# Down projection by 26 products of a 4x4 by 4x2 scheme, with gate and up products accumulated onto copies in PSUM

## The chip, the cores and the metric

One Trainium2 chip, one of its NeuronCores. A core has TensorE (PE, with PEld its weight loads), VectorE (DVE), ScalarE (ACT), GpSimd (POOL) and SyncE (SP, which issues most DMAs); they run their own instruction streams in order and meet through semaphores. The metric is the device time of one launch in microseconds.

## The reference

Two blocks read the same x (2048 tokens, 576 features); a sigmoid gate mixes them.

```python
B, S, D = 1, 2048, 576          # Df = 4608
x = A_x
g = sigmoid((x * gate_w).sum(-1, keepdims=True))
a = linear_attention(x, wqkv) @ wo      # 32 heads of 18
b = (gelu(x @ w_gate) * (x @ w_up)) @ w_down
return g * a + (1 - g) * b
```

All inputs and the result are float32.

## The kernel before

Float32 accuracy comes from splitting each operand into a high and a low part of type fp32r: `hi` is an ACT copy, `lo` is the raw value minus `hi`, made by DVE or POOL. A product is then hi·hi + hi·lo + lo·hi, three matmuls for each 128 rows of the contraction.

The program has three stages. The first (to about 243 us) is the attention block; it leaves g·a in DRAM (`ga_d`) and is written out step by step in the string `PLAN`. The second is **gate/up** (`gu_steps`, matmuls on L801), the third **down** (`unit`, matmuls on L1065). `manual_schedule` means that each engine's order is the order in which the Python code issues, so the order in the loops is the order on the chip.

*Gate/up.* The 2048 tokens are two halves p of 1024; each half is a 2x2 matrix of blocks (512 tokens by 288 features). The weight columns are taken 256 at a time, n = 0 to 17, again as 2x2 blocks. A **chain** (p, n, m), with m GATE or UP, multiplies the two by Winograd's scheme in 7 products (`PRODUCTS`), each of 7 matmuls of 128x512 into one PSUM bank. There are 72 chains (`CHAINS`), for each n in the order GATE half 0, GATE half 1, UP half 0, UP half 1, one after the other: `s1, s6, s7, s5, s2, s4, s3`. What the scheme adds between products is done by ACT and DVE on the way out: `s1` copies its bank to `p1` (L844), `s6` and `s7` add to it from their banks (L849, L863: `u2`, `u3`), `s5`, `s4`, `s3` add again (L835, L838), then GELU for GATE (L825, L855) or a multiplication into `es[i]` for UP (L828). So no product of PE waits for another engine, except for a free bank. `es` are four blocks of 512 tokens by 128 features; half 0 has `e...`, half 1 has `f`. After UP, four more sums (L877, L878, L879, L889) form the left operands of the down scheme, and `keep_block` (L831) stores all seven to DRAM (`h_d`).

Weights of the next n are fetched by SP (L805, 768 KB); POOL makes the four sums of the scheme (L321, 128x384 each), ACT the high parts (L815), POOL the low parts (L816, and 32 rows in L817). `w_split` and `w_fetch` stand behind the first product of a chain.

*Down.* h (1024 tokens of a half by 768 features) times the matching rows of w_down, as 2x2 by 2x2 blocks, again in 7 products: 6 steps s, 2 halves, 7 products, 84 **units**. A unit is four token tiles t of 9 matmuls, 128x288. Its left operand comes from DRAM (`h_load`, 768 KB) and is split by ACT and DVE (`h_make`, L966 and L967), three units ahead; its right operand is split by ACT and POOL (`d_make`, L946 and L948, in two pieces of 432) after POOL's `d_sum` (L953) made the scheme's sums. Each right operand serves both halves, so there are 42. Results go from PSUM into the accumulators `acc` in SBUF by DVE with the factor 1-g (L1073): `acc += bank * gate`, in 288 instructions; product 1 is copied to a second bank by ACT (L1069) and both are added to. In the sequence 1, 6, 2, 7, 5, 4, 3 the products use the banks a, b, a, b, d, b, d.

```python
    for u, (s, p, k) in enumerate(UNITS):
        unit(u, 0)          # token tiles 0, 1
        ...                 # h_make(u + 3), h_load(u + 6)
        unit(u, 1)          # token tiles 2, 3
```

## Time and profile before

| | |
|---|---|
| median of 3 runs | 1470.54 us (1469.54 to 1472.34) |
| the profiled execution (span) | 1470.6 us |
| busy: PE, PEld, DVE, ACT, POOL | 1465.0, 1311.9, 1038.5, 547.2, 720.9 us |
| gate/up stage | about 243 to 1066 us, 3528 matmuls of L801 |
| down stage | about 1066 to 1470.6 us, 3024 matmuls of L1065 |
| HBM | 156.84 MB read, 88.28 MB written |

The profile is one execution. Busy time of an engine is time in which an instruction of it ran; PEld overlaps PE. A group's row ends in `busy us, mean ns of one | idle time before them`, with what ended that idle time. A timeline row is `start, length, engine, line, operation, out<-in, count`.

### The profile page before, as it was taken

The page shows a single profiled execution, that of the slowest core. Times are in us where ns is not written, and L with a number is a line of the kernel's source. Part 1 is how long each engine was busy: PE and PEld are TensorE (multiplying, and loading weights), DVE is VectorE, ACT ScalarE, POOL GpSimd, SP SyncE. Part 2 cuts the span into 40 slices and gives each one's busy share as a digit, 9 for nine tenths or more (in the row PEclk, how much of TensorE's full clock was granted, in tenths as well). Part 3 has the DMA queues.
Part 4 walks back from the last instruction along what each step waited for, and adds up shares of the span by engine and source line. Part 5 has one row for each costly group of instructions (what it writes and reads, how often), then busy time and mean ns, then how long its engine had stood idle before and what let it go on. Part 6 is the DMA issues. An engine that isn't in the chain of part 4 may idle for free.

```text
span 1470.6 us, 21605 instructions
## 1 busy us (share of the span) xinstructions
PE 1465.0 (100%) x8312; PEld 1311.9 (89%) x8312; DVE 1038.5 (71%) x1351; ACT 547.2 (37%) x719; POOL 720.9 (49%) x522
## 2 busy tenths in 40 slices
PE   9999999999999999999999999999999999999999
PEld 9999899888888888888888888888899999999999
DVE  7887898565677655677665677665778777777775
ACT  7555656333322223222223222232254444443431
POOL 1664543456455464465464464462446464463710
PEclk9999999999999999999999999999999999999999
DMA  7564476653333222333222333224796655565563
GB/s 255 160 207 140 161 250 218 238 220 129 108 143 143 108 103 108 112 143 144 94 107 107 123 143 126 103 109 182 263 344 213 218 173 204 169 221 199 175 215 127
DMA packets 100599, 246.56 MB, mean 168 GB/s; under 512 B 9416, under 2 KB 36616, under 8 KB 98320
## 3 DMA queue, kind: packets, MB, share of 16 engines
q1 hardware_dynamic: 97760, 237.91, 46.6%
q10 hardware_dynamic: 2736, 7.28, 1.3%
q8 instruction: 65, 1.06, 0.3%
q14 instruction: 38, 0.31, 0.1%
HBM read 156.84 MB, written 88.28 MB: 167 GB/s over the span
## 4 chain that ended last, share of the span: by engine, by line
PE 98%; DMA 1%; DVE 1%; ACT 0%; SPq 0%; issue 0%; DVEq 0%
PE bank L801 54%; PE bank L1065 27%; PE bank L479 4%; PE pair L728 4%; PE pair L282 2%; PE kpair L282 2%; PE pair L237 2%; PE kpair L237 2%; PE den L667 1%; DMA xn<-xn 0%; DMA raw<-wk 0%; PE pair L634 0%; PE pair L530 0%; DVE e L246 0%; ACT pkh L252 0%
## 5 line engine op out<-in xcount | busy, mean ns | idle before, releaser
L801 PE MATMUL bank<-xo,wg 128*128 128x512 f32 x1764 | 403.7, 389 | 0.0
L801 PEld LDWEIGHTS bank<-xo,wg 128*128 128x128 f32 x1764 | 330.8, 188 | 68.9 <-DVE f L835 0.3
L801 PE MATMUL bank<-xo,wu 128*128 128x512 f32 x1715 | 391.8, 389 | 0.0
L801 PEld LDWEIGHTS bank<-xo,wu 128*128 128x128 f32 x1715 | 321.9, 188 | 66.8
L1073 DVE SCALAR_TENSOR_TENSOR acc<-bank,gate,acc 128x288 f32<-128x288 f32 x288 | 139.9, 512 | 67.1 <-PE bank L1065 64.8
L321 POOL TENSOR_TENSOR stage<-stage 128x384 f32<-128x384 f32 x132 | 153.7, 1185 | 49.0 <-ACT ga L735 23.2
L844 ACT ACTIVATE p<-bank 128x512 f32<-128x512 f32 x72 | 43.0, 597 | 325.2 <-PE bank L801 204.9
L816 POOL TENSOR_TENSOR wg<-stage,wg 128x768 fp32r<-128x768 f32 (+3 forms) x37 | 73.8, 1996 | 164.8 <-ACT wg L815 163.3
L816 POOL TENSOR_TENSOR wu<-stage,wu 128x768 fp32r<-128x768 f32 (+1 forms) x34 | 76.5, 2251 | 141.7 <-ACT wu L815 140.4
L1065 PE MATMUL bank<-wd,xo 128*128 128x288 f32 x1008 | 136.2, 295 | 0.0
L1065 PEld LDWEIGHTS bank<-wd,xo 128*128 128x128 f32 x1008 | 134.4, 188 | 0.0
L948 POOL TENSOR_TENSOR xo<-stage,xo 128x432 fp32r<-128x432 f32 x44 | 65.0, 1498 | 112.7 <-ACT xo L946 84.0
L849 DVE TENSOR_TENSOR u<-bank,p 128x512 f32<-128x512 f32 x72 | 49.4, 686 | 89.0 <-PE bank L801 81.2
L1065 PE MATMUL bank<-xo 128*128 128x288 f32 x792 | 107.0, 295 | 0.2 <-DVE u L838 0.2
L1065 PEld LDWEIGHTS bank<-xo 128*128 128x128 f32 x792 | 105.6, 188 | 0.5 <-DVE u L838 0.4
L948 POOL TENSOR_TENSOR wd<-stage,wd 128x432 fp32r<-128x432 f32 x40 | 59.4, 1510 | 90.1 <-ACT wd L946 72.3
L835 DVE TENSOR_TENSOR f<-bank,u 128x512 f32<-128x512 f32 x54 | 37.2, 691 | 69.2 <-PE bank L801 68.8
L825 ACT ACTIVATE f<-f 128x512 f32<-128x512 f32 x54 | 34.1, 632 | 128.6 <-DVE f L835 128.6
L863 DVE TENSOR_TENSOR u<-bank,u 128x512 f32<-128x512 f32 x72 | 49.8, 692 | 38.1 <-PE bank L801 34.1
L953 POOL TENSOR_TENSOR stage<-stage 128x432 f32<-128x432 f32 x48 | 76.3, 1616 | 0.0
L825 ACT ACTIVATE e<-e 128x512 f32<-128x512 f32 x54 | 34.0, 631 | 91.9 <-DVE e L835 91.9
L835 DVE TENSOR_TENSOR e<-bank,u 128x512 f32<-128x512 f32 x54 | 37.1, 691 | 40.4 <-PE bank L801 39.0
(198 smaller groups left out, 2373.2 us busy)
## 6 DMA issues: line engine op xcount, KB each, us to landing
h_d<-sx SPq DMA_DIRECT2D x108, 256.0 KB, 7.7
stage<-wgu SPq DMA_DIRECT2D x34, 768.0 KB
xo<-h_d SPq DMA_DIRECT2D x29, 768.0 KB, 6.9
e<-h_d SPq DMA_DIRECT2D x28, 768.0 KB, 4.2
hraw<-h_d SPq DMA_DIRECT2D x27, 768.0 KB, 4.1
h_d<-e SPq DMA_DIRECT2D x72, 256.0 KB, 2.0
h_d<-f SPq DMA_DIRECT2D x72, 256.0 KB, 2.0
stage<-wdn SPq DMA_DIRECT2D x6, 1728.0 KB, 9.6
```

Of the source, the lines that this page charges most:

```text
L237: nc.tensor.matmul(out_t[:, :n], xa, kvw[i][:, r, lo:lo + n], start=(k == 0), stop=(k == 13))
L282: nc.tensor.matmul(y[:, n, :KH], a, p[:, n * KH:(n + 1) * KH], start=(k == 0), stop=(k == len(ops) - 1))
L321: nc.gpsimd.tensor_tensor(o, a, b, OP.subtract)
L479: nc.tensor.matmul(ps[:wa.shape[1]], wa, xa, start=(k == 0), stop=(k == len(ops) - 1), skip_group_check=g == 4)
L801: nc.tensor.matmul(ps, w_, x_, start=start and i == 0, stop=i == 6, skip_group_check=not start)
L816: nc.gpsimd.tensor_tensor(w[:, i, 3:5], src[:, :, 0:2], f32(w[:, i, 0:2]), OP.subtract)
L825: nc.scalar.activation(es[i], es[i], AF.Gelu_apprx_tanh)
L835: nc.vector.tensor_tensor(es[i], a, b, OP.add)
L948: nc.gpsimd.tensor_tensor(w[:, 1, c], src[:, c], f32(w[:, 0, c]), OP.subtract)
L953: nc.gpsimd.tensor_tensor(draw[:, o, c], draw[:, x, c], draw[:, y, c], OP.subtract)
L1065: nc.tensor.matmul(y, h[:, hl, g, t * 128:(t + 1) * 128], w[:, wl, g * 288:(g + 1) * 288], start=k in (1, 5) and n == 0, stop=n == len(ops ...
L1073: nc.vector.scalar_tensor_tensor(o, y, gate[:, 1, st:st + 1], o, op0=OP.mult, op1=OP.add)
```

## The change

*Down* is now one scheme for a 4x4 matrix of left blocks (4 token blocks of 512 by 4 feature blocks of 384) and a 4x2 matrix of right blocks: 26 products, listed in the string `DOWN`, in three chunks c over the features (`NK = 3`, 1536 each), so 78 units of 36 matmuls. A line of `DOWN` gives the left operand (a sum of stored blocks `a`, `b`), the right operand, whether the product goes on in the banks of the one before (`c`), starts afresh (`-`) or starts on a copy of an earlier product's sum (a number, made by ACT), which outputs it is read into with which sign, and which right operands are summed just before. The chunks and the products that go on accumulate in PSUM, so a set of four banks is read only where the scheme needs it: 24 reads of four tiles, 96 DVE instructions (L1350). A negative read uses `probe[:, 8:]` (g-1), a negative left operand the factor -1 in `h_make` (L1204). Each unit has a right operand of its own: 78 splits on POOL (L1174, one piece of 864), and 54 sums of 864 (L1168), 33 on DVE and 21 on POOL, 18 tiles `vt` for them; the four newest right blocks are fetched ahead (`weight.fetch`).

*Every left operand is stored by the up steps.* UP of n even (role 0, "a" blocks) and of n odd (role 1, "b" blocks) belong together; `extras` forms the sums, a block at a time, in fixed slots after the UP chain, stores them (L1004, L1010) and, for role 1, loads back the "a" sums of the even n (L1007). The sums (L992, L995) read two SBUF blocks.

*Gate/up chains* no longer keep `u2`, `u3` in SBUF: `seed` has ACT copy bank a to a new bank b after `s1`, and b to a new bank c after `s6` (L939), and products 6, 3 accumulate onto b, products 7, 4 onto c. What is left to add is product 5, copied by ACT to `d_sum` (L967) and added by DVE (L969, L979 for GATE; L972, L982 for UP, back into PSUM). Two chains are interleaved in frames of seven slots:

```diff
+        def seed(name, src, k):
+            o = ps[name] = bank()
...
+                nc.scalar.activation(o, src, AF.Copy)
...
+        def s1():
+            a = ps["a"] = bank()
+            product(p, 1, w, a, True)
+            seed("b", a, 6)
+
+        def s6():
+            onto("b", 6)
+            seed("c", ps["b"], 7)
...
+        def s5():
+            d = bank()
+            product(p, 5, w, d, True)
+            nc.scalar.activation(d_sum, d, AF.Copy)
+            if m == GATE:
+                nc.vector.tensor_tensor(es[3], ps["c"], d_sum, OP.add)
+                gelu(3)
...
+    FRAME = 1, 7, 5, 3, 6, 2, 4
...
+                step = begun.get(frame if FRAME[i] in (1, 6, 2) else frame - 1, {}).get(FRAME[i])
```

The weight split of a chain stands in slot 0 of the frame before, the next fetch in its slot 5; the half-1 operand pieces move:

```diff
-    S_AT = [(0, 4), (1, 3), (2, 4), (2, 6), (3, 1), (3, 3)]
+    S_AT = [(0, 4), (2, 0), (3, 1), (3, 3), (3, 5), (4, 0)]
...
+    for n in range(3, NF2):
+        split_at(4 * n - 3, 0, GATE, *ALL)
+        fetch_at(4 * n - 3, 5, n, UP)
+        split_at(4 * n - 1, 0, UP, *ALL)
+        if n < NF2 - 1:
+            fetch_at(4 * n - 1, 5, n + 1, GATE)
```

The extras of an UP chain of half 1 with n odd (keys are frame, counted from the chain's own, and slot; `do` sums and stores, `get` loads), and those of the last chain that run in down, two groups a unit (`late`):

```diff
+        return {(-1, 5): [get("7", r0), get("x", r1), get("y", r2)],
+                (0, 3): [get("6", e[0])],
+                (0, 4): [get("5", e[3])],
+                (0, 5): [do(add, e[1], e[1], f[0])],
+                (0, 6): [do(add, e[1], e[1], r0, "a7b7")],
+                (1, 0): [do(sub, e[0], e[0], f[0], "a6b6"), do(add, r0, r0, f[0], "a7b6")],
+                (1, 1): [do(sub, r2, f[0], r2, "ayb6")],
+                (1, 2): [do(add, s0, s0, f[3])],
...
+                (2, 0): [do(sub, e[2], f[2], e[2]), do(add, e[2], e[2], r2, "a9b9")],
+                (2, 1): [do(add, s2, s1, f[3], "by"), get("8", r1)],
```

Down's tables and loop, each shortened to what the steps need:

```diff
+DOWN = """
+-b0 30 - -10 .
+-b2 r c . y=21-31,r=y-30
...
+NK = 3
...
+    def h_make(j):
...
+            if all(minus for minus, _, _ in DOWN[UNITS[j][0]].parts):
+                nc.scalar.activation(h[:, 0], raw, AF.Copy, scale=-1.0)
+                nc.vector.scalar_tensor_tensor(h[:, 1], raw, -1.0, f32(h[:, 0]), op0=OP.mult, op1=OP.subtract)
...
+        def make(self, j):
+            m, c = UNITS[j]
+            w, src = wd[j % 4], self.tile(DOWN[m].v, c)
+            nc.scalar.activation(w[:, 0], src, AF.Copy)
+            nc.gpsimd.tensor_tensor(w[:, 1], src, f32(w[:, 0]), OP.subtract)
...
+            for minus, i, j in d.reads:
+                st, o = 4 * i + t, acc[:, i, j, t]
+                by = probe[:, 8 + st:9 + st] if minus else gate[:, 1, st:st + 1]
+                nc.vector.scalar_tensor_tensor(o, y, by, o, op0=OP.mult, op1=OP.add)
...
+    weight.fetch(7)
+    h_load()
+    acc_load(1)
+    for u in range(len(UNITS)):
         unit(u, 0)
...
+        h_make(u + 3)
+        w_make(u + 3)
+        w_sums(u + 4)
+        later()
         unit(u, 1)
```

How the order moves, at three places. First PE in the middle of gate/up, before (x49 is a chain of seven products; xo and xo_3216 are the operands of half 0 and half 1, wg and wu the gate and up weights):

```order
L801 MATMUL bank<-xo,wg 128x512 x49
L801 MATMUL bank<-xo_3216,wg 128x512 x49
L801 MATMUL bank<-xo,wu 128x512 x49
L801 MATMUL bank<-xo_3216,wu 128x512 x49
L801 MATMUL bank<-xo,wg 128x512 x49
```

and after (xo_3263 is half 1's operand):

```order
L854 MATMUL bank<-xo_3263,wu 128x512 x7
L854 MATMUL bank<-xo_3263,wg 128x512 x21
L854 MATMUL bank<-xo_3263,wu 128x512 x14
L854 MATMUL bank<-xo_3263,wg 128x512 x7
L854 MATMUL bank<-xo,wg 128x512 x7
L854 MATMUL bank<-xo_3263,wu 128x512 x21
L854 MATMUL bank<-xo,wg 128x512 x14
```

Each chain is now spread over two frames: products 1, 6, 2 in its own, 7, 5, 3, 4 between those of the next chain.

Second DVE, from the end of an UP chain of half 1 into the next GATE chain, before (u and p are the sums in SBUF, sx the sums for down):

```order
L828 TENSOR_TENSOR f<-u_2892,f 128x512
L877 TENSOR_TENSOR sx<-f 128x512
L878 TENSOR_TENSOR sx<-sx,f 128x512
L879 TENSOR_TENSOR f<-f 128x512
L838 TENSOR_TENSOR u_2891<-bank,u_2891 128x512
L828 TENSOR_TENSOR f<-u_2891,f 128x512
L889 TENSOR_TENSOR sx<-f,sx 128x512
L849 TENSOR_TENSOR u_2891<-bank,p_2890 128x512
L863 TENSOR_TENSOR u_2892<-bank,u_2891 128x512
L835 TENSOR_TENSOR e_3212<-bank,u_2892 128x512 x2
```

and after, for n odd (mid holds d_sum, r0 and r1, r is r2, e_3256 is half 0's blocks):

```order
L992 TENSOR_TENSOR mid<-mid,sx 128x512
L992 TENSOR_TENSOR f<-f 128x512
L932 TENSOR_TENSOR f<-bank,f 128x512
L995 TENSOR_TENSOR mid<-mid,f 128x512
L995 TENSOR_TENSOR e_3256<-f,e_3256 128x512
L992 TENSOR_TENSOR e_3256<-e_3256,r 128x512
L992 TENSOR_TENSOR sx<-sx,f 128x512
L969 TENSOR_TENSOR e_3256<-bank,mid 128x512
L979 TENSOR_TENSOR e_3256<-bank,mid 128x512
L992 TENSOR_TENSOR sx<-r,f 128x512
L995 TENSOR_TENSOR r<-sx,r 128x512
```

The GATE sums (L969, L979), for which ACT's GELU waits, now stand behind the operand sums of the UP chain before.

Third DVE in the middle of down, before, where half 0 ends and half 1 begins (xo and hraw are buffers of the left operands here, acc_8625 and acc_8626 the accumulators of the halves):

```order
L1073 SCALAR_TENSOR_TENSOR acc_8625<-bank,gate,acc_8625 128x288 x4
L967 TENSOR_TENSOR xo<-e_3212,xo 128x1536
L1073 SCALAR_TENSOR_TENSOR acc_8625<-bank,gate,acc_8625 128x288 x2
L967 TENSOR_TENSOR xo<-hraw,xo 128x1536
L1073 SCALAR_TENSOR_TENSOR acc_8626<-bank,gate,acc_8626 128x288 x2
L967 TENSOR_TENSOR xo<-xo 128x1536
```

and after:

```order
L1350 SCALAR_TENSOR_TENSOR acc<-bank,probe,acc 128x288 x2
L1204 SCALAR_TENSOR_TENSOR xo<-wg,xo 128x1536
L1168 TENSOR_TENSOR stage<-f,vt_8792 128x864
L1204 SCALAR_TENSOR_TENSOR wu<-wg,wu 128x1536
L1168 TENSOR_TENSOR vt_8794<-sx,stage 128x864
L1350 SCALAR_TENSOR_TENSOR acc<-bank,gate,acc 128x288 x4
```

There are fewer reads of PSUM, sums of right operands stand between the low parts of h, and a bank that goes on is read in two pairs around them.

More of the change, by code (lines that the diff above doesn't have):

```diff
@@ new lines, in tile_gated_mix, with w_sums, w_make, h_load @@
+    weight = Weights()
+    AHEAD = 4
+    def w_sums(j, ahead=AHEAD):
+        if j < len(UNITS):
+            weight.fetch(j + ahead)
+            weight.sums(j)
+    def w_make(j):
+        if j < len(UNITS):
+            weight.make(j)
+    loads, raw_of = deque(range(len(UNITS))), {}
+    def h_load():
+        while loads and raw_free:
+            j = loads.popleft()
+            m, c = UNITS[j]
+            raw_of[j] = raw_free.popleft()
+            nc.sync.dma_start(raw_at[raw_of[j]], h_d[c][:, m])
@@ L1032, in tile_gated_mix @@
+    assert not plan
     both.close()
```

508 lines of the change are left out of this document (327 added, 181 removed).

## The prediction

> **What bounds the kernel now.** I read the page first (span, busy shares, chain), then PE's waits, then the stages as stretches.
>
> ```profile
> span 1470.6 us, 21605 instructions
> PE 1465.0 (100%) x8312; PEld 1311.9 (89%) x8312; DVE 1038.5 (71%) x1351; ACT 547.2 (37%) x719; POOL 720.9 (49%) x522
> PE 98%; DMA 1%; DVE 1%; ACT 0%; SPq 0%; issue 0%; DVEq 0%
> PE bank L801 54%; PE bank L1065 27%; PE bank L479 4%; PE pair L728 4%; PE pair L282 2%; PE kpair L282 2%; PE pair L237 2%; PE kpair L237 2%; PE den L667 1%; DMA xn<-xn 0%; DMA raw<-wk 0%; PE pair L634 0%; PE pair L530 0%; DVE e L246 0%; ACT pkh L252 0%
> ...
> PE bank L1065 <- DVE u L838: 0.2, 1, 0.2
> ...
> 243.00:1066.00 823.00, 823.00 (x3703) 685.12 (x3702) 539.58 (x668) 233.26 (x311) 423.05 (x293) 1.00 0.39 140
> 1066.00:1470.60 404.60, 401.15 (x3024) 400.56 (x3023) 294.94 (x376) 168.93 (x169) 182.25 (x118) 1.00 0.60 205
> ```
>
> PE is the chain from end to end. After 243 us its whole list of waits is one row of 0.2 us. The last two rows are the gate/up stage and the down stage (columns: length, then busy us of PE, PEld, DVE, ACT, POOL, then clock, DMA share, GB/s). The clock is 1.00. So a matmul removed is worth its full slot, and whatever makes PE wait is paid in full, since today nothing does. The profiled execution has 1470.6 us, the median of the runs 1470.54, so no correction lies between them.
>
> **Term 1, fewer matmuls in down.** Two rows by source line, L801 (gate/up) and L1065 (down), over the whole span, PE first:
>
> ```profile
> 0.00:1470.60 1470.60, 800.48 (x3528) 661.89 (x3528) 1.00 0.48 168
> 0.00:1470.60 1470.60, 401.34 (x3024) 400.93 (x3024) 1.00 0.48 168
> ```
>
> Down had 84 units of 36 matmuls (3024); now 26 products in 3 chunks are 78 units, 2808 matmuls of the same shape. 401.34/3024 = 0.1327 us each, a unit is 4.78 us, and 216 x 0.1327 = **-28.7**; down alone is then 372.7. Gate/up keeps its 3528 matmuls at 0.2269: a product of seven is 1.59 us, a frame of seven products 11.1.
>
> **Term 2, seeds and sums in gate/up.** ACT now copies bank to bank twice a chain (one such copy of 512 is some 0.60, as L844 below), about +140 x 0.60 = 84 us on an engine busy 233 of 823: beside PE, which needs a seed three products (4.8 us) after its source. DVE loses work: 648 instructions of 128x512 become 577. But they bunch. At every second feature group (odd n from 3 to 15, seven times) three frames in a row, from that of the UP chain of half 1 on, hold 6, 10 and 6 operand sums, each with both inputs in SBUF. What such a sum costs beside POOL:
>
> ```profile
> 599.67 0.69 DVE L877 TENSOR_TENSOR sx<-f 128x512 f32<-128x512 f32 x1
> 603.05 2.23 DVE L889 TENSOR_TENSOR sx<-f,sx 128x512 f32<-128x512 f32 x1
> 605.20 0.68 DVE L849 TENSOR_TENSOR u<-bank,p 128x512 f32<-128x512 f32 x1
> 588.40 1.39 DVE L877 TENSOR_TENSOR sx<-e 128x512 f32<-128x512 f32 x1
> ...
> 602.63 2.10 POOL L816 TENSOR_TENSOR wu<-stage,wu 128x768 fp32r<-128x768 f32 x1 [9.12 <-ACT wu L815]
> 604.81 1.34 POOL L817 TENSOR_TENSOR wu<-stage,wu 32x384 fp32r<-32x384 f32 x1
> 580.48 1.86 POOL L816 TENSOR_TENSOR wg<-stage,wg 128x768 fp32r<-128x768 f32 x1 [10.45 <-ACT wg L815]
> 582.41 1.00 POOL L817 TENSOR_TENSOR wg<-stage,wg 32x384 fp32r<-32x384 f32 x1
> 606.23 2.41 POOL L816 TENSOR_TENSOR wu<-stage,wu 128x1024 fp32r<-128x1024 f32 x1
> 608.72 1.29 POOL L817 TENSOR_TENSOR wu<-stage,wu 32x512 fp32r<-32x512 f32 x1
> 610.36 4.06 POOL L321 TENSOR_TENSOR stage<-stage 128x384 f32<-128x384 f32 x4 [0.35 <-DMA stage<-wgu]
> ...
> 606.18 0.33 SPq L805 DMA_DIRECT2D stage<-wgu  x1
> ...
> L844 ACT ACTIVATE p<-bank 128x512 f32<-128x512 f32 x72 | 43.0, 597 | 325.2 <-PE bank L801 204.9 <-DVE sx L877 120.3
> L825 ACT ACTIVATE e<-e 128x512 f32<-128x512 f32 x54 | 34.0, 631 | 91.9 <-DVE e L835 91.9
> ```
>
> Alone a sum is 0.69; started while POOL runs it is 2.23, until POOL's 2.10 is over, and 1.39 beside the shorter L321 operations. With an input in PSUM it stays 0.68. Now the walk, t = 0 at the start of the first of the three frames. DVE's burst starts when the previous chain's s5 is done and copied: 3 x 1.59 + 0.6 = 5.4. Up to the GATE sum into es[1] in the third frame stand 12 + 15 + 5 = 32 instructions, at 0.68 in a row 21.8: 27.2. PE needs the c seed of the next GATE chain after 22 products, at 34.9; behind es[1] ACT has one GELU (0.63) and the seed (0.60). So 34.9 - 1.2 - 27.2 = 6.5 us may be lost to POOL. POOL in that stretch: the second half of one split (2.41+1.29); four weight sums (4.06), whose fetch now stands in slot 5, on SP behind a store that waits for DVE until 11, so that POOL has them at 15.4 (606.18 to 610.36 is 4.2); a whole second split (1.86+1.00+2.41+1.29) from 25.6; 14.3 in all. Down DVE's row of instructions, its sums meet 2 of the first (lost 1.5), 3 of the weight sums (2.2), and, since DVE is in the last frame late, all four of the second split (5.4): 9.1, or 2.6 too many. If DVE arrives 1.5 earlier, two sums slip in ahead of the 1.86, and nothing is late. I take the middle of the two, some 1.15 a time: 7 x 1.15 = **+8**; bounds 0 (there is no wait to win back) and 7 x (14.3 - 6.5) = 55.
>
> The Trainium skill, "SBUF — State Buffer", Who interferes with whom, has this as an exclusive lock on a port pair that VectorE and GpSimd share, taken by a VectorE instruction with two SBUF inputs against a GpSimd one that reads SBUF, for the whole instruction. The 2.23 against 0.69 agrees; what its "whole" would mean for down stands behind the third rival.
>
> **Term 3, start of gate/up.** Chain 2 now begins four products sooner, while its weights come as before:
>
> ```profile
> 270.68 6.51 PE L801 MATMUL bank<-xo,wg 128*128 128x512 f32 x28
> ...
> 284.22 0.33 SPq L805 DMA_DIRECT2D stage<-wgu  x1
> 288.13 0.32 SPq L807 DMA_DIRECT2D stage<-ws_d  x1
> ...
> 292.87 1.49 ACT L815 ACTIVATE wu<-stage 128x1536 fp32r<-128x1536 f32 x1 [1.30 <-DMA stage<-ws_d]
> ```
>
> ACT stands at that second transfer until 292.9; behind it now queue three split pieces of 384 (1.4 in all, an estimate from 1.49 for 1536), d_sum and the c seed of chain 2 (0.6 each), done at 295.5. PE wants that seed 15 products after 270.7, at 294.5. With as much again for the half-1 operands, whose last two pieces (s_make) move from frame 3 into frames 3 and 4, just ahead of their use, **+2**; bounds 0 (transfers a little sooner) and 5.
>
> **Term 4, start of down.** DVE's first units carry the last extras. Rows:
>
> ```profile
> stage<-wdn SPq DMA_DIRECT2D x6, 1728.0 KB, 9.6
> ...
> 1226.79 1.75 DVE L967 TENSOR_TENSOR xo<-e,xo 128x1536 fp32r<-128x1536 f32 x1
> 1231.56 2.18 DVE L967 TENSOR_TENSOR wu<-hraw,wu 128x1536 fp32r<-128x1536 f32 x1
> ...
> 1231.00 1.13 POOL L953 TENSOR_TENSOR stage<-stage 128x432 f32<-128x432 f32 x1
> ...
> L1073 DVE SCALAR_TENSOR_TENSOR acc<-bank,gate,acc 128x288 f32<-128x288 f32 x288 | 139.9, 512 | 67.1 <-PE bank L1065 64.8
> ```
>
> The first weight fetch is four tiles, as many bytes as the 9.6 us row: the first pair at about 4.8, the second at 9.6. A DVE weight sum of 864 lies between 0.69 (512) and 1.75 (1536): 1.05. DVE: pair of sums 4.8 to 6.9, two extras 8.3, low part of h 10.0, pair 12.1, four extras 14.8, port waits 2: it reads product 0's first bank at 17.3. Product 1 goes on in that bank and wants it at 3 units, 14.3. PE waits 3.0, and 1.1 more on the third bank behind the next h: **+4**; bounds 0 (tiles sooner, no port waits) and 8.
>
> **Term 5, bank to bank in down.** Products now follow each other in the same four banks, where before another product stood between. The third bank is done at 3.58 of the last chunk's unit and wanted at 7.16. Between its reads DVE does the low part of h (1.75) and at five places a weight sum: 3.1 + 1.75 + 1.05 + one port wait of 0.5 to 2 + 0.51 = 6.9 to 8.4. Five times up to 1.3: 0 to 6, I take **+2**. The reads fall from 288 to 96 (-98 us of DVE), which is what makes this room.
>
> At nothing: stores and loads of the extra operands go from 252 to 366 DMAs of 256 KB in gate/up, at a DMA share of 0.39; SP's queue waits with DVE, not PE with SP; without that cover DVE would wait for a store before it rewrites es[3]. The splits now start one frame ahead of their first use instead of two: ACT 0.6 + 1.1, POOL 1.86 + 1.00 after the first product make 6.2 of 11.1. If POOL is 5 later there, PE waits for W. The tail stays two reads of 0.51 and a store. POOL's and ACT's down work rises (42 weight splits become 78), hidden as long as POOL keeps within 3 units of lookahead.
>
> Sum: -28.7 + 8 + 2 + 4 + 2 = -12.7, so 1470.6 - 12.7 = **1458**.
>
> **Rivals.**
> - *Nothing waits.* All of terms 2 to 5 near 0: 1442 to 1447. For it: DVE has 71 instructions fewer, and PE's waits today are 0.2. Against: the room of 6.5 and the 9.1 counted.
> - *Slower: DVE's burst.* If POOL costs DVE over 6.5 + 4.1 = 10.6 us in each of the seven stretches, 7 x 4.1 eats the 28.7. The place is the same GATE sum into es[1]. At 12 it is 1470.6 - 28.7 + 7 x 5.5 + 8 = 1488. For it: POOL has 14.3 there, and a store that holds es[3] adds to it. Against: 13 of the 32 instructions read PSUM and let POOL pass.
> - *The port binds down* (POOL and DVE exclude each other there, as in term 2). POOL: 78 splits and 21 sums of 864; the 768 and 1024 rows give 2.15 ns an element, so 2.07 each, 204.9. DVE: 78 x 1.75 + 33 x 1.05 = 171. Together 376, over the 372.7 of PE, where before (84 x 1.75 + 132 x 1.13 = 296) 401 were at hand. Then down takes 376 and more where sums bunch: 1462 to 1473. Against: the 2.18 row started 0.56 after POOL's 1.13 and lost 0.43, so an operation holds about 0.14 less than its row; 210 x 0.14 = 29 less is 347, which fits.
>
> By the lock of the Trainium skill ("SBUF — State Buffer", Who interferes with whom), held for whole instructions, it would be the 376, so 1458 + 3.5 = 1461; by the row it is 347, and 1458 stays.
>
> **Numbers.** Forecast (1447 to 1467) 0.53; nothing waits 0.22; port binds down 0.14, a third of it within 0.2% of before (2.9 us, about what a measurement tells from no change); slower 0.11. Faster: 0.53 + 0.22 + 0.09 = 0.84; same 0.05; slower 0.11. The range 1444 to 1472 leaves out the best tenth and the slower case.
>
> **What would show it.** L1340 at 2808 matmuls and some 373 us. In PE's waits: a row on ACT (the seed L939) some seven times for term 2, with DVE es sums (L969, L979) waited for by ACT; a row on DVE L1350 once near the start of down for term 4 and a few under 1.3 for term 5. Prediction wrong: no PE wait on ACT in gate/up (then 1442 to 1447), or one of over 4 in each stretch, or DVE's L1168 and L1207 far over 1.05 and 1.75 with h or w late (PE waiting on POOL L1174).

## The result: 1534.4 us, slower by 4.3%

The kernel after takes 1534.42 us (median of 4 runs, 1533.54 to 1537.65), the kernel before 1470.66 (median of 4): ratio 1.0431, 95% interval 1.0415 to 1.0447. The forecast was 1458, faster. The profiled execution of after has 1531.8 us. Its page, and the two rows by source line (L854 gate/up, L1340 down; PE's busy time first):

```profile
span 1531.8 us, 21118 instructions
PE 1460.6 (95%) x8096; PEld 1296.4 (85%) x8096; DVE 959.5 (63%) x1121; ACT 640.4 (42%) x863; POOL 784.0 (51%) x505
```

```profile
0.00:1531.80 1531.80, 812.08 (x3528) 665.84 (x3528) 0.98 0.54 184
0.00:1531.80 1531.80, 384.90 (x2808) 381.19 (x2808) 0.98 0.54 184
```

The matmuls did go: 2808 in down, PE's instructions down by 216. But PE now stands idle for 1531.8 - 1460.6 = 71.2 us, against 5.6 before, and its matmuls are busy longer than their slots: L854 11.6 us more than before, L1340 384.9 against 372.7. The account: +65.6 idle, -28.7 matmuls, +24.3 slower matmuls (11.6, 12.2 and 0.5 elsewhere) is +61.2, the whole difference of the spans. By stage (length, busy PE, PEld, DVE, ACT, POOL, then clock, DMA share, GB/s):

```profile
243.00:1066.00 823.00, 804.11 (x3592) 665.77 (x3591) 429.99 (x558) 305.31 (x447) 390.99 (x296) 1.00 0.46 158
1066.00:1110.00 44.00, 31.03 (x113) 23.86 (x113) 31.18 (x38) 12.28 (x16) 6.20 (x3) 0.83 0.92 319
1110.00:1531.80 421.80, 384.44 (x2807) 380.40 (x2806) 294.64 (x217) 177.78 (x162) 271.55 (x96) 0.96 0.63 214
```

Idle are 18.9 us in gate/up up to 1066, 13.0 in its last 44 us, 37.4 in down. PE's waits (us, times, longest), where before had one row of 0.2:

```profile
PE bank L1340 <- DVE acc L1350: 32.2, 10, 7.2
PE bank L854 <- DVE e L969: 9.9, 7, 2.8
PE bank L854 <- DVE bank L972: 8.0, 2, 5.1
PE bank L854 <- ACT bank L939: 4.4, 2, 3.7
PE bank L854 <- POOL xo L1225: 3.9, 1, 3.9
PE bank L854 <- DVE f L969: 3.5, 1, 3.5
...
PE bank L1340 <- POOL xo L1174: 1.9, 2, 1.4
PE bank L854 <- ACT sx L937: 1.7, 1, 1.7
```

Five places, read by their times. *The handovers*, seven times, one of them:

```profile
719.04 2.73 POOL L869 TENSOR_TENSOR wu<-stage,wu 128x1024 fp32r<-128x1024 f32 x1
...
719.44 2.89 DVE L992 TENSOR_TENSOR sx<-sx,f 128x512 f32<-128x512 f32 x1
722.25 0.68 DVE L969 TENSOR_TENSOR e<-bank,mid 128x512 f32<-128x512 f32 x1
...
722.98 1.89 PE L854 MATMUL bank<-xo,wg 128*128 128x512 f32 x7 [1.17 <-DVE e L969]
```

A DVE sum, 0.69 alone, begins 0.4 after POOL's piece of 1024 and is over 0.56 after that piece (722.33 against 721.77); L969 stands behind it, and PE waits: its next product (4 of the GATE chain) adds onto the bank that L969 reads. *Down*, in a run of units whose right operand is summed on POOL:

```profile
1345.59 2.06 POOL L1174 TENSOR_TENSOR xo<-stage,xo 128x864 fp32r<-128x864 f32 x1 [1.04 <-ACT xo L1173]
1347.60 3.59 POOL L1168 TENSOR_TENSOR vt<-vt,f 128x864 f32<-128x864 f32 x1
1352.22 2.06 POOL L1174 TENSOR_TENSOR xo<-vt,xo 128x864 fp32r<-128x864 f32 x1 [1.04 <-ACT xo L1173]
1354.24 3.57 POOL L1168 TENSOR_TENSOR stage<-vt,stage 128x864 f32<-128x864 f32 x1
...
1351.22 0.93 ACT L1173 ACTIVATE xo<-vt 128x864 fp32r<-128x864 f32 x1 [4.33 <-POOL vt L1168]
1352.05 1.48 ACT L1206 ACTIVATE xo<-xo 128x1536 fp32r<-128x1536 f32 x1
...
1353.56 2.34 DVE L1207 TENSOR_TENSOR xo<-xo 128x1536 fp32r<-128x1536 f32 x1 [3.44 <-ACT xo L1206]
```

This is a ring of three engines. POOL's low part starts at 1345.59 and again at 1352.22: 6.63 us a unit, where PE needs 4.78. ACT's high part of w waits for POOL's sum, the high part of h stands behind it on ACT, DVE's low part of h waits for that, and POOL's next sum (1354.24) begins 0.68 after that low part and ends 1.91 after it is over (1355.90). Six units in a row lose six times 1.85 us, which eats the lookahead: at 1333 PE is in unit 41 (counted from 0) and 44 right operands are ready, at 1365.4 it is in unit 48 and 49 are. Then PE waits, and the wait carries the name of the reads (L1350), because these stand behind the low part of h, and here a sum, on DVE. *The end of gate/up*, where ACT waits for a left operand of down:

```profile
1077.38 1.49 ACT L1203 ACTIVATE xo<-xo 128x1536 fp32r<-128x1536 f32 x1 [6.25 <-DMA xo<-h_d]
1078.77 0.58 ACT L929 ACTIVATE f<-bank 128x512 f32<-128x512 f32 x1
1079.25 0.92 ACT L1173 ACTIVATE xo<-stage 128x864 fp32r<-128x864 f32 x1
1080.07 0.58 ACT L939 ACTIVATE bank<-bank 128x512 f32<-128x512 f32 x1
```

Behind it stand a GELU (L929), a high part of w (L1173) and the seed L939, onto which a later product of PE adds. *The start* has three waits (L937, L972, L1225), and *down's first units* one of 7.2.

Last, the clock. Around one long wait and around a short one (same columns as above):

```profile
1360.00:1365.00 5.00, 5.00 (x39) 4.95 (x38) 3.20 (x3) 0.68 (x2) 4.43 (x2) 1.00 0.39 123
1365.00:1370.00 5.00, 0.72 (x6) 0.48 (x4) 3.20 (x2) 1.77 (x2) 4.53 (x2) 0.84 0.85 326
1370.00:1375.00 5.00, 2.65 (x11) 2.65 (x12) 4.40 (x4) 3.11 (x3) 3.82 (x3) 0.50 0.97 335
1375.00:1380.00 5.00, 5.00 (x39) 5.00 (x39) 5.00 (x3) 2.42 (x2) 2.91 (x2) 0.98 0.82 282
...
900.00:905.00 5.00, 3.81 (x18) 2.81 (x17) 4.96 (x6) 1.32 (x3) 4.10 (x2) 1.00 0.38 123
```

After a wait of some 7 us the clock is 0.50, and 11 matmuls take 2.65 us, 0.24 each instead of 0.13. Where 1.2 us is lost (900 to 905) it stays at 1.00. So a long wait costs its length and 1 to 3 us more.

### The profile page after: what moved, and what is told of

It is laid out like the page before. It is cut to its first block, busy times and chain, and to the rows that moved or that the text cites. A ratio compares the mean times of both kernels' runs of the same rounds, so it can differ in the third digit from the quotient of the medians.

```text
span 1531.8 us, 21118 instructions
## 1 busy us (share of the span) xinstructions
PE 1460.6 (95%) x8096; PEld 1296.4 (85%) x8096; DVE 959.5 (63%) x1121; ACT 640.4 (42%) x863; POOL 784.0 (51%) x505
## 5 line engine op out<-in xcount | busy, mean ns | idle before, releaser
L854 PE MATMUL bank<-xo,wg 128*128 128x512 f32 x1764 | 419.8, 391 | 17.8 <-DVE e L969 9.9
L854 PE MATMUL bank<-xo,wu 128*128 128x512 f32 x1715 | 405.7, 390 | 4.6 <-DVE bank L972 2.9
L854 PEld LDWEIGHTS bank<-xo,wg 128*128 128x128 f32 x1764 | 331.1, 188 | 90.5 <-DVE e L969 12.8
L854 PEld LDWEIGHTS bank<-xo,wu 128*128 128x128 f32 x1715 | 323.2, 189 | 72.9 <-DVE bank L972 3.3
L1340 PE MATMUL bank<-xo 128*128 128x288 f32 x2124 | 294.7, 300 | 28.9 <-DVE acc L1350 27.0
L1340 PEld LDWEIGHTS bank<-xo 128*128 128x128 f32 x2124 | 289.6, 192 | 32.4 <-DVE acc L1350 16.8
L939 ACT ACTIVATE bank<-bank 128x512 f32<-128x512 f32 x139 | 80.9, 582 | 242.1 <-PE bank L854 238.5
L1174 POOL TENSOR_TENSOR xo<-vt,xo 128x864 fp32r<-128x864 f32 x42 | 107.7, 2564 | 78.5 <-ACT xo L1173 76.1
L1174 POOL TENSOR_TENSOR xo<-stage,xo 128x864 fp32r<-128x864 f32 x26 | 68.5, 2635 | 103.2 <-ACT xo L1173 90.6
L869 POOL TENSOR_TENSOR wu<-stage,wu 128x768 fp32r<-128x768 f32 (+3 forms) x38 | 75.7, 1993 | 84.1 <-ACT wu L868 82.5
L972 DVE TENSOR_TENSOR bank<-bank,mid 128x512 f32<-128x512 f32 x36 | 25.1, 697 | 142.7 <-ACT mid L967 142.7
L1340 PE MATMUL bank<-xo,wu 128*128 128x288 f32 x684 | 96.1, 299 | 5.2 <-DVE acc L1350 5.2
L1340 PEld LDWEIGHTS bank<-xo,wu 128*128 128x128 f32 x684 | 93.6, 192 | 5.8 <-issue 3.6
L969 DVE TENSOR_TENSOR f<-bank,mid 128x512 f32<-128x512 f32 x18 | 12.4, 691 | 118.5 <-ACT mid L967 114.2
L967 ACT ACTIVATE mid<-bank 128x512 f32<-128x512 f32 x71 | 42.4, 597 | 96.8 <-PE bank L854 88.6
L1173 ACT ACTIVATE xo<-vt 128x864 fp32r<-128x864 f32 x42 | 38.7, 921 | 81.3 <-POOL vt L1168 53.6
L781 PEld LDWEIGHTS pair<-kw,p 128*128 128x128 f32 x448 | 60.8, 189 | 1.0
L781 PE MATMUL pair<-kw,p 128*128 128x288 f32 x448 | 61.4, 295 | 0.0
```

What stands on the lines that cost most here:

```text
L781: nc.tensor.matmul(y[:, i, :288], p[:, 5 * a + g], KW[g][:, wl, i * 288:(i + 1) * 288], start=(n == 0), stop=(n == 13))
L854: nc.tensor.matmul(ps, w_, x_, start=start and i == 0, stop=i == 6, skip_group_check=not start)
L869: nc.gpsimd.tensor_tensor(w[:, i, 3:5], src[:, :, 0:2], f32(w[:, i, 0:2]), OP.subtract)
L939: nc.scalar.activation(o, src, AF.Copy)
L967: nc.scalar.activation(d_sum, d, AF.Copy)
L972: nc.vector.tensor_tensor(d, ps["c"], d_sum, OP.add)
```

## The experiments

Below, PE's waits are counted from the starts of its matmuls: every step from one start to the next over 0.5 us, less 0.2 for the matmul itself, by place (in the text a single wait is the whole step). All but after, best_a, best_b and best_c have one time each; I read no difference under 3 us from these. Kernel before: 1472.3 to 1472.9 beside them.

| kernel | time | start | handovers | end of gate/up | down, first 60 us | down, later |
|---|---|---|---|---|---|---|
| after | 1534.4 | 9.5 | 11.2 | 14.8 | 7.3 | 28.0 |
| d_dve | 1511.6 | 8.8 | 11.3 | 13.0 | 8.7 | 10.8 |
| d_half | 1534.4 | 10.0 | 11.7 | 13.7 | 6.9 | 28.5 |
| d_read | 1526.9 | 9.3 | 13.0 | 14.9 | 9.3 | 17.8 |
| d_both | 1502.7 | 11.6 | 11.9 | 14.8 | 9.5 | 0.0 |
| hand | 1524.0 | 10.4 | 0.0 | 14.3 | 7.7 | 27.7 |
| d_late | 1514.4 | 8.5 | 11.5 | 15.9 | 3.2 | 13.9 |
| gu_ends | 1535.3 | 9.1 | 12.4 | 16.0 | 3.0 | 30.1 |
| all_d | 1501.9 | 8.6 | 0.0 | 17.4 | 0.6 | 15.2 |
| all_read | 1488.7 | 10.3 | 0.0 | 20.4 | 5.8 | 1.4 |
| all_raw | 1479.8 | 5.4 | 0.0 | 8.3 | 8.8 | 6.3 |
| all_raw2 | 1480.9 | 5.9 | 0.0 | 17.1 | 2.6 | 2.6 |
| spread_a | 1472.4 | 4.8 | 0.0 | 9.4 | 4.1 | 4.2 |
| best_a | 1472.0 | 5.6 | 0.0 | 3.8 | 10.5 | 3.9 |
| best_b | 1474.9 | 5.4 | 0.0 | 3.9 | 12.4 | 3.9 |
| best_c | 1465.5 | 5.2 | 0.0 | 6.0 | 2.9 | 3.6 |

### Down: the ring, the port, the order

**d_dve.**

```diff
-                eng = nc.vector if len(DOWN[m].parts) == 1 else nc.gpsimd
+                eng = nc.vector
```

> Down's 21 sums of right operands that POOL makes go to DVE too; nothing else moves. Theory A (a ring of three engines: POOL's sum of 3.57 us, then ACT's high part, then POOL's low part of 2.06, one after the other, 6.6 us a unit where PE needs 4.78; the low part of h and then the reads of a bank stand behind it): POOL keeps only its 78 x 2.06 = 161 us, the ring opens, DVE gets some 21 x 1.05 to 1.5 = 22 to 32 us more of 419; the waits of PE for L1350 fall from 32.2 to under 15, time 1495 to 1515. Theory B (the port that DVE and POOL share is full; each instruction holds it whole): the port's work falls by 21 x (2.07 - 1.05) = 21 us, time 1510 to 1520, and DVE's sums stay near 2.9. Theory C (the reads of a bank only stand too far back in DVE's own order): with more ahead of them on DVE it gets worse, 1540 or more.

**d_half.**

```diff
-                eng.tensor_tensor(self.tile(name, c), a, b, OP.add if op == "+" else OP.subtract)
+                t = self.tile(name, c)
+                for s in ((slice(0, 432), slice(432, 864)) if eng is nc.gpsimd else (slice(0, 864),)):
+                    eng.tensor_tensor(t[:, s], a[:, s], b[:, s], OP.add if op == "+" else OP.subtract)
...
-            nc.gpsimd.tensor_tensor(w[:, 1], src, f32(w[:, 0]), OP.subtract)
+            for o in (0, 432):
+                nc.gpsimd.tensor_tensor(w[:, 1, o:o + 432], src[:, o:o + 432], f32(w[:, 0, o:o + 432]), OP.subtract)
```

> Each of POOL's instructions in down on 128x864 (78 low parts, 21 sums) is cut into two of 432, as the kernel before had them; nothing else moves. Theory B in its sharp form (what hurts DVE is the length of one hold of the port): DVE's sums fall from 2.9 to about 1.9 and its low parts of h from 2.3 to 2.0, PE's waits for L1350 halve, time 1510 to 1522. Theory A (ring): POOL's own time does not fall (2 x 1.12 = 2.24 against 2.06 for the low part), ACT can start no sooner, so the ring stays at 6.6 or more: 1530 to 1550.

**d_read.**

```diff
-        h_make(u + 3)
         w_make(u + 3)
         w_sums(u + 4)
         later()
         unit(u, 1)
+        h_make(u + 3)
         later()
```

> In down the making of h (ACT high, DVE low) is issued behind the second half of a unit, not between its halves: a bank's second pair of reads stands right behind the first on DVE, and on ACT the high part of w comes ahead of the high part of h. Theory C (order on DVE): the waits for L1350 go, time 1495 to 1510. Theory A (ring): the reads no longer wait for ACT's high part of h, but the ring of POOL and ACT keeps its 6.6 us; what was a wait for L1350 becomes a wait for w (POOL L1174) or h, time 1515 to 1535.

d_dve: 1511.6, 22.9 less; its row of the reads, and below it that of d_read:

```profile
PE bank L1340 <- DVE acc L1350: 18.8, 8, 8.6
```

```profile
PE bank L1340 <- DVE acc L1350: 25.5, 6, 9.2
```

The ring's number (1495 to 1515) held, though 18.8 is more than the 15 it allowed, 8.7 of it at down's start. The port's number (1510 to 1520) holds too, and DVE's sums did stay at 2.9, so this run alone does not part the two. d_half speaks against the length of one hold: DVE's sums did fall from 2.9 to 1.97, as that theory said, but the time did not change (1534.4), and POOL's two halves of a sum take as long as the whole did:

```profile
1353.34 1.11 POOL L1177 TENSOR_TENSOR xo<-vt,xo 128x432 fp32r<-128x432 f32 x1
1354.41 3.70 POOL L1170 TENSOR_TENSOR stage<-vt,stage 128x432 f32<-128x432 f32 x2
...
1353.59 2.47 DVE L1210 TENSOR_TENSOR xo<-xo 128x1536 fp32r<-128x1536 f32 x1 [3.56 <-ACT xo L1209]
```

The first half waits for DVE's low part like the whole sum, so the length of POOL's hold is not what costs. Halving leaves the port's total work as it was, so d_half says nothing of a port that is full; d_read and d_both do. The port is one link of the ring: it adds 1.66 us to POOL's own 1.91, and ACT and DVE wait for the sum. d_read won 7.5 by order alone, with the same work on the port, within the ring's 1515 to 1535 and not order's 1495 to 1510; POOL's unit stayed at 6.6 us (1342.92, 1349.55, 1356.16), as the ring had it, but the waits kept the name L1350, where the ring's theory had them move to w or h. The order of DVE's own queue costs something, but it is not the main thing.

**d_both**, the two together.

> Only the two edits of down: all sums of right operands on DVE (d_dve), and the making of h behind the second half of a unit with w ahead of it (d_read). Separately they gave 23.0 and 7.5. If both act on the one ring of POOL, ACT and DVE (reads and ACT's part of the ring), down goes from 419 to 383 to 390 and the time to 1500 to 1507, more than either alone and more than their sum of 30.5 or about it; if d_read only repeats what d_dve gave, 1509 to 1512.

1502.7: 31.7 won, as good as the sum of 22.9 and 7.5. Down's waits are one, at its start:

```profile
PE bank L1340 <- DVE acc L1350: 9.4, 1, 9.4
```

```profile
1173.00:1498.00 325.00, 324.76 (x2450) 324.51 (x2448) 274.21 (x201) 152.62 (x138) 165.19 (x65) 1.00 0.62 215
```

From 60 us into down on, PE is busy 324.76 of 325 us at a clock of 1.00: these two edits remove the 28.0, and the slow matmuls with them. The port has the same work as in d_dve (DVE's sums stay at 2.9), where 10.8 us of waits were left, so it was not full: it costs PE nothing once nothing waits in a ring and the reads come sooner.

### The handovers

**hand.**

```diff
-        split_at(4 * n - 1, 0, UP, *ALL)
+        split_at(4 * n - 1, 0, UP, ALL[0], *(() if n % 2 == 0 else ALL[1:]))
+        if n % 2 == 0:
+            split_at(4 * n - 1, 3, UP, ALL[1])
```

> In gate/up, at the seven UP splits that fall into the burst of DVE sums, the second block (ACT 128x1536, POOL 1024 and 32x512) is moved from slot 0 to slot 3 of the same frame. Theory of the prediction (a DVE sum of two SBUF operands that runs beside POOL's 1024 piece takes 2.89 instead of 0.69, and L969 stands behind it): the seven waits of 1.56 go, -10.9: 1522 to 1526. Rival (DVE's own count of instructions is what is late, or the frame's fetch): the waits stay at 1.5 each, 1532 to 1537.

1524.0, 10.4 less, and the row on `e L969` is gone. So the split's second block beside the burst made the seven waits. The run moves the block whole (ACT's high part, POOL's 1024 and its 32x512); that it is the piece of 1024 is read from rows as above, where DVE's sum takes 2.89.

### The ends of gate/up: order or bytes

**d_late**, d_dve and:

```diff
-        if late:
+        if late and u >= 2:
```

> As d_dve (all sums of right operands on DVE, 1511.6), and the last operand sums of gate/up, which run in down's first units, begin at unit 2 and not at unit 0, so that none stands ahead of the first reads of a bank. Theory (down's start is late by DVE's order: four such sums and two port waits stand ahead of the first L1350, PE waits 8.9 at 1132.9): the wait falls to 0 to 3, 1503 to 1506. Rival (the start is late by the transfers of the right blocks, 7.3 us from issue to landing at a DMA share over 0.85): the sums of units 3 and 4 stay as late, 1509 to 1512.

1514.4, no gain. The first wait did fall, from 8.9 to 2.4 and 1.2, so the late extras made it; but a wait of 5.1 came 50 us later, and down took as long as in d_dve (396.8 and 397.1 from its first matmul to its last). A miss for both theories.

**gu_ends**, with d_late's line too (shortened):

```diff
-... else (slice(32, 64), kt, nc.gpsimd)
+... else (slice(32, 64), kt, nc.vector)
-    S_AT = [(0, 4), (2, 0), (3, 1), (3, 3), (3, 5), (4, 0)]
+    S_AT = [(0, 4), (1, 3), (2, 4), (2, 6), (3, 1), (3, 3)]
-            if c < LAST or (frame, i) in ((0, 3), (0, 4), (0, 5), (0, 6), (1, 0), (1, 1)):
+            if c < LAST or (frame, i) in ((0, 3), (0, 4), (0, 5), (0, 6)):
-(LAST - 1, 1, lambda: h_load()) ... (LAST - 1, 4, lambda: h_make(0)) ... (LAST, 2, lambda: h_make(1))
+(LAST - 1, 4, lambda: h_load()) ... (LAST, 0, lambda: h_make(0)) ... (LAST, 5, lambda: h_make(1))
```

> Both ends of gate/up, down's sums as in the kernel after. Start: all low parts of half 1's operand on DVE (the last two were on POOL, behind weight sums), and its pieces made in the slots of the kernel before. End: the first left operand of down is fetched three slots later (slot 4 of the frame before the last, with the second weight pair) and made four slots later, behind the loads that the last extras wait for; the extras of slots (1, 0) and (1, 1) of the last chain, and all that follow, run in down from unit 2 on. Theory (order: ACT and DVE stand in a queue at an instruction that waits for a transfer, and what PE needs stands behind it): the start's 10 us fall to 2 to 5, the end's 14 to 2 to 6, down's first wait of 7.5 to 0 to 4: 1512 to 1520. Rival (bandwidth: 331 GB/s and a DMA share of 0.96 at the end, the data cannot come sooner): only the start is won, the end's waits move by some us but stay 12 or more: 1523 to 1529.

**all_d** and **all_read**, the combinations without and with d_read.

> All of d_dve, hand, gu_ends and d_late together, the late extras behind the second half of a unit. If the places are independent, their gains add: d_dve -23, hand -10.5, gu_ends and d_late -14 to -24 together: 1477 to 1487. If what is won at one place is waited for at the next (bandwidth, or DVE as the one engine that everything stands on), 1490 to 1500.

> As all_d, and in down the making of h is issued behind the second half of a unit, with w ahead of it, as in d_read. If the reads still stand behind low parts of h, sums and their port waits on DVE (19 us of waits for L1350 in d_dve), 4 to 10 less than all_d. If the ring with POOL alone made d_read's gain of 7.5, the same as all_d within 2.

gu_ends: 1535.3, a miss; the end got no better (16.0). all_d 1501.9 fits neither "1477 to 1487" nor "1490 to 1500"; all_read is 13.1 less than all_d, more than the 4 to 10 expected, and all of it in down (396.8 to 382.5 from first to last matmul), where all_d's waits were still 13.6 on the reads. The end of gate/up grew to 20.4, and ACT's rows in all_read say why moving `h_make` by some slots did not help:

```profile
1073.11 1.48 ACT L1203 ACTIVATE xo<-xo 128x1536 fp32r<-128x1536 f32 x1 [5.73 <-DMA xo<-h_d]
1074.50 0.58 ACT L967 ACTIVATE mid<-bank 128x512 f32<-128x512 f32 x1
...
1094.12 1.48 ACT L1203 ACTIVATE wu<-xo 128x1536 fp32r<-128x1536 f32 x1 [8.02 <-DMA xo<-h_d]
```

One raw buffer passes from one left operand to the next, so each load begins only when the operand before is made, and ACT stands 6 to 8 us at its high part; I had only put other work (the copies of product 5, L967) behind it.

**all_raw**: the first three left operands are loaded into the low half of their own buffers; at the start the pieces of half 1's operand are made some slots sooner (not shown).

```diff
+    def h_first(j):
+        m, c = UNITS[j]
+        nc.sync.dma_start(f32(hb[j][:, 1]), h_d[c][:, m])
...
+            raw = f32(h[:, 1]) if j < 3 else raw_at[at]
...
+(LAST - 1, 3, lambda: h_first(0)), (LAST, 1, lambda: h_first(1)), (LAST, 3, lambda: h_first(2))
```

> As all_read in down and at the handovers; both ends of gate/up changed once more, after the traces of gu_ends and all_read: there ACT stood 5.7, 3.1 and 8.0 us at the high part of a left operand of down whose 768 KB had been asked for 5 to 7 us before, and the copies that PE's next products need stood behind it. Now the first three left operands are loaded straight into the low half of their own buffers (no one raw buffer that passes from one to the next), each asked for 6 to 8 slots of 1.59 us ahead of its high part and behind the loads of the extras. Start: pieces of half 1's operand some slots sooner, the tsum split behind the copy of product 5. Theory (order on ACT and DVE, with a transfer of 5 to 8 us under a DMA share of 0.9): end of gate/up from 20.4 to 3 to 8, start from 10.3 to 4 to 7: 1467 to 1478. Rival (bandwidth: the bytes cannot come sooner): the end stays at 15 or more, 1483 to 1488.

**all_raw2**, against all_raw:

```diff
-            if c < LAST or (frame, i) in ((0, 3), (0, 4), (0, 5), (0, 6)):
+            if c < LAST or (frame, i) in ((0, 3), (0, 4), (0, 5), (0, 6), (1, 0), (1, 1)):
```

> As all_raw, but the extras of slots (1, 0) and (1, 1) of the last chain stay in gate/up as in the kernel after. They wait for loads issued 4 us before (DVE idle 3.3 at 1105 in the kernel after), and L972 stands behind them: theory of order, 3 to 6 us more at the end of gate/up than all_raw and down's start some 1 to 2 less: 1469 to 1482. By bandwidth the same as all_raw within 2.

all_raw: the end falls to 8.3 and the start to 5.4, but 9.3 us come back in down (391.8 from its first matmul to its last, 382.5 in all_read): 1479.8, just above the range. all_raw2 has 8.8 more at the end of gate/up and 10.5 less in down (381.3), and ends at 1480.9. What is won at one end is lost at the other, as it would be in a stretch that is bound as a whole; by what, these two runs do not show. Two stretches of all_raw across the seam:

```profile
1050.00:1100.00 50.00, 39.89 (x209) 34.08 (x208) 33.56 (x40) 15.03 (x18) 6.79 (x4) 0.93 0.91 328
1100.00:1150.00 50.00, 43.18 (x308) 42.98 (x309) 42.91 (x37) 21.36 (x22) 22.82 (x9) 0.90 0.93 336
```

**spread_a** and **spread_b** take bytes out of these 100 us (spread_b calls `later` once a unit, from unit 1 on). Not shown: spread_a also loads the first left operands some slots sooner, makes them later, and moves weight fetches, so it changes order too.

```diff
-(LAST - 4, 6, lambda: w_sums(0, 2))
+(LAST - 4, 6, lambda: w_sums(0, 3))
-        if u in (1, 3, 6):
-            acc_load((0, 2, 3)[(1, 3, 6).index(u)])
+        if u in (0, 6, 11, 17):
+            acc_load((1, 0, 2, 3)[(0, 6, 11, 17).index(u)])
```

> As all_raw, with the same bytes spread: the second weight pair of down is fetched four frames earlier, the first left operands a few slots earlier, three of the four accumulator blocks as late as unit 6, 11 and 17 (were 1, 3, 6), the raw left operands of units 4 and 5 behind the first weight fetch. The first h is made behind both GATE sums. If bytes bind (330 GB/s and a share of 0.92 over these 100 us), the end of gate/up falls from 8.3 to 3 to 6 and down's first 60 us from 8.8 to 2 to 5: 1470 to 1475. If order alone binds, only the first does: 1476 to 1479.

> As spread_a, with the late extras one group a unit from unit 1 on, in place of two from unit 2 on. If DVE's load in units 3 to 12 makes the wait of 5.7 at 1157 in all_raw, that falls under 2 and the time by 2 to 4 against spread_a; if a transfer makes it, no change.

spread_a: 1472.4, 7.4 less than all_raw, in the range for bytes; but the end of gate/up stayed (9.4), and what fell was down (391.8 to 384.7); since it changes order too, it does not show that bytes bind. spread_b: 1484.2, the wrong way, with a wait of 12.8 that ends at 1162; in it right blocks are loaded over `f` and `sx` before the last sums that read these, so those sums are of other numbers, and I draw nothing else from it.

**best_a** and **best_b**, the last waits by order; best_a against spread_a, then best_b's addition (shortened):

```diff
-(LAST, 6, lambda: h_make(1)) ... (LAST + 1, 3, lambda: h_make(2))
+(LAST + 1, 3, lambda: h_make(1)) ... (LAST + 1, 6, lambda: h_make(2))
-            if c < LAST or (frame, i) in ((0, 3), (0, 4), (0, 5), (0, 6)):
+            if c < LAST or (frame, i) in ((0, 3), (0, 4), (0, 5)):
+        if u == 3:
+            later(u)
...
-    raw_free.extend((1, 2))
-    h_load()
+    h_load()
+    acc_load(1)
+        if u == 0:
+            raw_free.extend((1, 2))
+            h_load()
```

> As spread_a; the high parts of h for units 1 and 2 are made after the copies and sums of the last products of gate/up, and the last chain's extras of slots (0, 5) and (0, 6), which wait for a load, run in down, one group more in unit 3. If order binds there, the wait of 7.1 at 1079.7 falls to 0 to 2 and down starts no later: 1465 to 1469. If bytes bind, the wait goes to down's first units: 1470 to 1473.

> As best_a, and in down's first units the left operands of units 3 to 5 are loaded behind the first weight tiles and the first accumulator block, those of 4 and 5 behind unit 0. If the 4.3 at 1101 in spread_a came from the weight tiles being late (5.0 us of DVE's wait), it falls under 2: 1 to 3 less than best_a. If left operands are late in their place: 1 to 5 more.

best_a: 1472.0, ratio 1.0001 (0.9992 to 1.0010): the end fell to 3.8, down's first units rose to 10.5, the number of the theory of bytes. best_b: 1474.9, ratio 1.0017 (1.0008 to 1.0026), within the 1 to 5 more of left operands that are late in their place. SyncE's row in best_a shows where it was given back, and PE what it waited for:

```profile
1073.18 0.55 SPq L1004 DMA_DIRECT2D h_d<-mid  x1
1080.77 0.32 SPq L1010 DMA_DIRECT2D mid<-ha_d8x  x1
1081.18 0.38 SPq L1010 DMA_DIRECT2D r<-ha_d8y  x1
1081.62 0.42 SPq L1200 DMA_DIRECT2D xo<-h_d  x1
1082.13 1.82 SPq L1157 DMA_DIRECT2D vt<-wdn  x4
...
1100.96 11.22 PE L1347 MATMUL bank<-xo 128*128 128x288 f32 x64 [10.38 <-ACT xo L1207]
```

For 7.6 us SyncE issues nothing: it stands at the load into `mid`, whose last content is still being stored and read, with the next left operand and the weight tiles behind it.

**best_c**: those two loads behind the weight tiles, and the left operand of unit 3 asked for one slot sooner.

```diff
-                put(LAST + 1, 0, does[1])
-                put(LAST + 1, 0, does[2])
+                gets = does[1:]
...
-(LAST + 1, 0, lambda: raw_free.append(0)), (LAST + 1, 0, h_load)
+(LAST, 6, lambda: raw_free.append(0)), (LAST, 6, h_load)
...
     weight.fetch(5)
     raw_free.extend((1, 2))
     h_load()
+    for do in gets:
+        do()
+    acc_load(1)
```

> As best_a, with SyncE's order changed around the start of down: the left operand of unit 3 and the first weight tiles are asked for ahead of the two loads (mid and r from the kept a sums) that wait for a store, the first accumulator block right behind them. In best_a SyncE has no issue from 1073.2 to 1080.8. Order on SyncE: the weight tiles come when the operand that lay in their place is done with (about 1078, was 1082) and the wait of 10.7 at 1101 falls to 1 to 5: 1461 to 1468, ratio 0.992 to 0.997. Bytes: 3.8 MB at 330 GB/s are 11.5 us from 1078 on, so the last of them lands no sooner than 1090 in any order, the wait stays at 7 or more: 1469 to 1472.

1465.5 (1464.3 to 1467.4), ratio to the kernel before 0.9959, 95% interval 0.9945 to 0.9972: the scheme of 26 products beats the kernel before by 0.4%. The wait of 10.7 became 3.1, as order had it (1 to 5, 1461 to 1468), and the bytes did come sooner, 331 and 355 GB/s in the two stretches across the seam where best_a had 309 and 326:

```profile
1050.00:1100.00 50.00, 42.24 (x221) 36.59 (x220) 41.62 (x47) 20.42 (x22) 15.05 (x6) 0.93 0.93 331
1100.00:1150.00 50.00, 46.52 (x341) 46.31 (x340) 46.85 (x39) 22.44 (x22) 28.16 (x10) 0.97 0.97 355
1150.00:1462.50 312.50, 309.34 (x2343) 308.90 (x2341) 262.07 (x191) 145.70 (x132) 158.70 (x63) 1.00 0.63 218
```

So order on SyncE holds a part at the seam: best_c shows it, 6.4 us less than best_a. Order on ACT moved the wait in all_raw, but of the 12.1 won at the end 9.3 came back in down. That bytes bind is not shown; at a share of 0.93 to 0.97 little more may be left to win by order, which is argued and not measured. How much of the last 17.7 us of waits are bytes stays open.

## Why the prediction was wrong

**Term 1 (-28.7) was right**: in best_c a step between matmuls of down has a median of 0.132 us, and 2808 of them are there. But it supposed a clock of 1.00. In after L1340 was busy 12.2 us over its slots, and PE 24.3 in all, which is in no term.

**Term 2 (+8): the burst, the port and the size right, the path wrong.** Seven waits, 11.2 in the place of 8 (six of 1.4, one of 3.0, where I took 1.15), behind an operand sum that ran beside "the second split"; hand took them away. But PE did not wait for the seed behind es[1] and its GELU: none of the seven is on L939, the row on ACT that was to show the term. It waited for the GATE sum into es[3] (L969), since product 4 adds onto the bank that this sum reads, and that product comes after 20 products, not 22: due at 689.91 + 31.8 = 721.7, begun at 722.98. The seed that I walked to was done at 724.67, 34.8 after 689.91 and inside my 34.9, so the walked path gives no wait in this one. That the size came so near is in part luck.

**Term 3 (+2, bounds 0 and 5), mis-sized: 9.5.** The 295.5 that I worked out for ACT's copies held nearly (L967 of product 5 runs at 295.83), but PE waited 2.9 there, for the DVE sum L972 behind it, where I took 1; 1.7 at 281 on L937 is in no term. Most of the rest are the pieces of half 1's operand, to which I gave 1: moved later, the last two came from DRAM at 315.6 and then met POOL, and PE waited 3.9 on them until 323.3:

```profile
314.42 4.05 POOL L373 TENSOR_TENSOR stage<-stage 128x384 f32<-128x384 f32 x4 [8.52 <-DMA stage<-wgu]
318.55 4.65 POOL L1225 TENSOR_TENSOR xo<-f,xo 32x1024 fp32r<-32x1024 f32 x2
```

**Term 4 (+4, bounds 0 and 8)**: 7.3, inside, at the place that I walked to (the start of product 1's first unit, 3 units in) and by the order on DVE: d_late, without the extras there, has 3.2.

**Term 5 (+2, bounds 0 to 6), with POOL's and ACT's work in down put at nothing beside it, is the step that failed: 28.0.** I counted DVE's instructions between two reads, each with one port wait, and took POOL and ACT for cover: "hidden as long as POOL keeps within 3 units of lookahead". It does not keep within them. The sum of unit u+4 is issued just ahead of its own split, so sum, ACT, split and the low part of h that shares the port make one ring, 2.06 + 1.66 + 1.91 + 0.92 = 6.55 us (6.63 measured) against 4.78. A chain's length in one unit had to be compared with PE's unit, not the engines' totals with the stage. d_dve, which opens the ring, takes 17.2 of the 28.0 away; the other 10.8 go only when the reads come sooner on DVE too (d_both). The prediction's own sign of being wrong came, L1168 far over 1.05: 25 of after's 33 sums on DVE took about 2.9. One of its rows (shortest, median, longest in ns):

```profile
L1168 DVE TENSOR_TENSOR vt<-vt,vt x9: 1045/2904/2916, 1116.6 to 1504.0; 128x864 f32<-128x864 f32 x9
```

**The rival "the port binds down"** came nearest to the cause, with 0.14 and 1462 to 1473. Its total was right: by the runs' durations without a wait, 99 x 2.05 on POOL and 78 x 1.75 + 33 x 1.05 on DVE are 374 against my 376. The discount ("an operation holds about 0.14 less than its row") held too. A sum of POOL takes 2.04 alone, the shortest of this row of d_read:

```profile
L1168 POOL TENSOR_TENSOR vt<-vt,vt x8: 2042/3560/3570, 1207.2 to 1452.5; 128x864 f32<-128x864 f32 x8
```

In the ring's rows it ends 1.91 after DVE's low part, and in the handover DVE's sum of 0.69 ends 0.56 after POOL's piece: 0.13 less each. The Trainium skill, "SBUF — State Buffer", Who interferes with whom, has the loser blocked for the whole instruction; the trace agrees to within that 0.13. d_half shows what pieces change: DVE's sums behind POOL get shorter, POOL's sum behind DVE's low part does not (3.70 against 3.57). So the total was not what failed, by the row or by whole instructions (1461): it did not bind, and the price failed because that work comes in runs of up to six units and ACT is in the ring.

**Not in the sum at all: the end of gate/up, 14.8.** I gave term 4 the extras on DVE, and did not ask what stands on ACT and SyncE in the last 44 us, where the loads of left operands, kept sums and weights meet at a DMA share of 0.92. "SP's queue waits with DVE, not PE with SP" was said for gate/up's middle at a share of 0.39; it was not checked where the share is more than twice that.

**The rival "slower: DVE's burst"** (1488) had the right sign and the wrong place: the burst cost 11.2 in waits, not the 38 that it reckoned.

## What to carry over

Where several in-order engines hand one unit of work on to each other, add up the chain of one unit, with every hold of a shared port in it, and compare that with the unit of the engine that must not wait; busy totals over a stage, and a lookahead, hide it. Where two stages meet, list for each queue what stands behind its first instruction that waits for a transfer: the wait that PE shows names the last link (here the reads), the cause was three links earlier. A scheme that takes matmuls away pays only while no wait is left to eat the gain: the same 26 products gave 1534, 1503 and 1466 us by the order, the engines and the buffers around them.

## What I had not expected of the hardware

A wait of PE costs more than its length when it is long: behind the waits of 3.7, 5.5, 6.9 and 7.5 us in after's down, 12 to 21 matmuls ran at over 1.15 of their slot, 1.4 to 2.7 us lost each time, the clock at 0.50; behind those of 1.7 to 2.3 one matmul did, 0.1 us. All in all PE was busy 24.3 us longer than its matmuls' slots, in the granted clock 0.83 at the end of gate/up and 0.96 in down. In best_c the clock is 1.00 from 1150 on. The Trainium skill, "TensorE: Matmul & The Clock Gate", Why this matters for your kernels, asks for no idle of PE over about 3 us between bursts; the trace agrees with that bound as far as it shows it (the clock stays at 1.00 behind 2.2 and falls behind 3.7; behind a wait of 3.2 in gate/up it stayed in after and was 0.51 in d_both from 633.1 to 640.0), and prices it.
